# Windowed attention and a two-product feed-forward block: the first product of nine of the twelve pairs of token blocks as seven products of half sums, and two pairs at once while the weights arrive

## The chip, the cores and the metric

One core of one Trainium2 chip runs the whole program. The metric is device time of the program in microseconds. Three runs of the kernel before gave 628.5, 630.02 and 631.56 us, median 630.02 us. One further execution was profiled; all rows below come from it.

## The reference, cut to what matters

```python
# 4 batches, 8 heads, 768 tokens, head size 64; d_model 512, d_ff 2048; all float64 weights, float32 q, k, v
scores = q @ k.T / 8 - slope[h] * dist          # kept: 8 global columns and the 96 tokens up to the row's own
a = exp(scores - max); a = a / (sum(a) + 1e-9)
x = (a @ v)                                     # 4 * 768 = 3072 tokens of 512
h = x @ w_in                                    # 512 -> 2048
g = where(h >= 1, h, where(h <= -1, 0, (h + 1)**2 / 4))
out = g @ w_out                                 # 2048 -> 512, float32
```

## The kernel before, in words

The 3072 tokens are 24 units of 128; two units are a pair (c = 0 to 11, 256 tokens). Units 0 to 3 are the first blocks of the four batches; they see only themselves and go through a float32 path (`first_scores` to `first_x`). The other 20 units look at two blocks of 128 keys and go through a float16 path in two halves of four heads each (`put_unit`).

Every float16 product is made of three: an operand is the sum of a high and a low float16 part, and high*high, high*low and low*high are summed in PSUM.

The weights are float64 in memory. Each of 32 pieces (16 of `w_in`, 16 of `w_out`, 128 columns or rows of d_ff each) is loaded raw, turned into float32 by three integer steps on VectorE (`w_bits`, L480, L484, L487), split by two steps of ScalarE (`w_hi` L500, `w_scale` L507) and one of GpSimd (`w_lo` L514).

`ffn1(c, g)` is the first product of a pair: for a group g of 256 columns of d_ff (eight groups), 24 matmuls with a weight block of 128x128 and 256 moving columns (tokens), L885. `gelu(c, g, s)` makes g of it in five steps on 512 columns: ScalarE L898, VectorE L903 and L908, ScalarE L912, GpSimd L916. `ffn2(c, t, f)` is a step of the second product: three matmuls of 512 moving columns for token block t and piece f of `w_out` (L928), 32 steps a pair. `finish` scales and stores the result. `scores` (24 matmuls, L757) and `attend` (24, L800) are the attention products of half a unit; transposes of units 4 to 23 are done by DMA (`turn_p`, `turn_x`).

All work is put in a plan with `at(time, function, ...)`, and the list `PLACE` gives the order in which the functions are issued; each engine runs its instructions in that order. `PLACE` leaves some planned fillers out: a filler (`warm`, L443) is a matmul of zeros with 512 columns that nobody reads. 109 of them are issued, up to 74 us. In the order of before, pair 0's first product runs while `w_in` arrives, pair 0's second and pair 1's first while `w_out` arrives, and then, pair by pair, the second product of pair c is interleaved with the first of pair c + 1 and the attention of two units of a later pair. The 128 `check_reduce` of the weights (L546) are spread over the second half. Checks on the value ranges end in a flag that chooses a general path.

## Time and profile before

| | |
|---|---|
| median of three runs | 630.02 us |
| span of the profiled execution | 629.1 us |
| what lies around the span, by the median | 0.9 us |
| TensorE busy | 615.7 us, 98% of the span |
| VectorE, ScalarE, GpSimd busy | 448.0, 418.7, 239.5 us |
| granted clock of TensorE over the span | 0.999 |

"Busy" counts an instruction from its start to its modelled end, so that matmuls which follow each other overlap; the distance from one start to the next is what a matmul costs in a stream. The same holds for VectorE and ScalarE, whose instructions overlap by some 0.1 us.

### The profile page before, as it was taken

The page shows a single profiled execution, that of the slowest core. Times are in us where ns is not written, and L with a number is a line of the kernel's source. Part 1 is how long each engine was busy: PE and PEld are TensorE (multiplying, and loading weights), DVE is VectorE, ACT ScalarE, POOL GpSimd, SP SyncE. Part 2 cuts the span into 40 slices and gives each one's busy share as a digit, 9 for nine tenths or more (in the row PEclk, how much of TensorE's full clock was granted, in tenths as well). Part 3 has the DMA queues.
Part 4 walks back from the last instruction along what each step waited for, and adds up shares of the span by engine and source line. Part 5 has one row for each costly group of instructions (what it writes and reads, how often), then busy time and mean ns, then how long its engine had stood idle before and what let it go on. Part 6 is the DMA issues. An engine that isn't in the chain of part 4 may idle for free. (4 is left out here: it accounts for less than half of the span.)

```text
span 629.1 us, 14881 instructions
## 1 busy us (share of the span) xinstructions
PE 615.7 (98%) x5665; PEld 420.8 (67%) x5665; DVE 448.0 (71%) x1150; ACT 418.7 (67%) x1070; POOL 239.5 (38%) x226
## 2 busy tenths in 40 slices
PE   7999999899999999999999999999999999999996
PEld 4676666556876767767757667667667767767652
DVE  6889999987676656665777777777777686663440
ACT  4778898997777776676686776766866765632220
POOL 0336786650544424433443333425324421122210
PEclk9999999999999999999999999999999999999999
DMA  6847566597533553464395497586476455361121
GB/s 201 261 144 225 187 227 221 129 170 157 126 87 77 91 121 93 80 148 111 69 231 154 94 208 186 127 186 175 110 177 183 112 140 137 76 150 69 51 69 38
DMA packets 144227, 88.08 MB, mean 140 GB/s; under 512 B 108180, under 2 KB 124820, under 8 KB 144148
## 3 DMA queue, kind: packets, MB, share of 16 engines
q1 hardware_dynamic: 144000, 86.92, 55.4%
q8 instruction: 46, 0.75, 0.5%
q14 instruction: 33, 0.27, 0.1%
q10 hardware_dynamic: 148, 0.13, 0.1%
HBM read 54.53 MB, written 6.29 MB: 97 GB/s over the span
## 5 line engine op out<-in xcount | busy, mean ns | idle before, releaser
L885 PE MATMUL h<-xt,wih 128*128 128x256 f16 x1536 | 256.4, 273 | 1.0 <-DVE u L908 0.9
L916 POOL TENSOR_TENSOR gl<-u,gh 128x512 f16<-128x512 f32 x96 | 117.4, 1224 | 284.9 <-ACT gh L912 274.6
L885 PE MATMUL h<-xt,wil 128*128 128x256 f16 x768 | 209.4, 273 | 0.0
L885 PEld LDWEIGHTS <-wih 128*128 128x128 f16 x1536 | 147.4, 98 | 30.9 <-DVE u L908 1.6
L928 PE MATMUL o<-wol,gh 128*128 128x512 f16 x384 | 145.6, 379 | 1.3 <-POOL wol L514 1.2
L928 PE MATMUL o<-woh,gh 128*128 128x512 f16 x384 | 145.8, 380 | 0.0
L928 PE MATMUL o<-woh,gl 128*128 128x512 f16 x384 | 145.6, 379 | 0.0
L928 PEld LDWEIGHTS <-gh 128*128 128x128 f16 x768 | 71.8, 98 | 67.3
L903 DVE SCALAR_TENSOR_TENSOR h<-h,u 128x512 f32<-128x512 f32 x96 | 66.7, 694 | 68.2 <-ACT u L898 68.0
L590 ACT ACTIVATE z<-z,nm 128x256 f32<-128x256 f32 (+1 forms) x192 | 91.7, 479 | 14.9 <-DVE nm L578 14.3
L912 ACT ACTIVATE gh<-u 128x512 f16<-128x512 f32 x96 | 60.2, 627 | 60.4 <-DVE u L908 60.1
L898 ACT ACTIVATE u<-h,half 128x512 f32<-128x512 f32 x96 | 64.9, 676 | 43.3 <-PE h L885 43.2
L578 DVE CUSTOM_DVE_ANT_0 z<-s,bias 128x256 f32<-128x256 f32 (+1 forms) x192 | 67.2, 396 | 26.6 <-PE s L757 23.2
L885 PEld LDWEIGHTS <-wil 128*128 128x128 f16 x768 | 75.0, 98 | 8.8
L775 DVE SCALAR_TENSOR_TENSOR ph<-z,ph 128x1024 f16<-128x1024 f32 x40 | 60.0, 1499 | 22.1 <-ACT ph L773 21.8
L928 PEld LDWEIGHTS <-gl 128*128 128x128 f16 x384 | 37.5, 98 | 47.2 <-issue 2.2
L908 DVE SCALAR_TENSOR_TENSOR u<-u,h 128x512 f32<-128x512 f32 x96 | 65.3, 681 | 3.3 <-DVE good L298 0.3
L546 DVE TENSOR_REDUCE sq<-c_raw 128x1 f32<-128x256 f32 x128 | 48.6, 408 | 0.2
L773 ACT ACTIVATE ph<-z 128x1024 f16<-128x1024 f32 x40 | 42.0, 1050 | 0.7
L757 PEld LDWEIGHTS <-qh 64*128 64x128 f16 x960 | 26.9, 94 | 16.7 <-issue 9.5
L800 PEld LDWEIGHTS <-pt 128*128 128x128 f16 x960 | 33.4, 98 | 7.0
L590 ACT ACTIVATION_READ_ACCUMULATOR z<-z,nm 128x1 f32 x192 | 36.0, 187 | 0.0
(101 smaller groups left out, 676.6 us busy)
## 6 DMA issues: line engine op xcount, KB each, us to landing
w_raw<-in_moe_w_in_dram SPq DMA_DIRECT2D x16, 512.0 KB, 3.8
w_raw<-in_moe_w_out_dram SPq DMA_DIRECT2D x16, 512.0 KB, 3.7
c_raw<-in_moe_w_in_dram SPq DMA_DIRECT2D x32, 256.0 KB, 3.5
c_raw<-in_moe_w_out_dram SPq DMA_DIRECT2D x32, 256.0 KB, 3.1
vr<-in_v_dram SPq DMA_DIRECT2D x28, 256.0 KB, 3.5
kr<-in_k_dram SPq DMA_DIRECT2D x28, 256.0 KB, 3.7
qr<-in_q_dram SPq DMA_DIRECT2D x24, 256.0 KB, 4.0
out_dram<-ob SPq DMA_DIRECT2D x23, 256.0 KB, 3.0
```

The costliest lines, as they stand in the source:

```text
L546: nc.vector.tensor_reduce(sq[:, col : col + 1], tops[n, e], axis=AX.X, op=op, apply_absolute_value=True)
L578: nc.vector.tensor_tensor_reduce(out=p32[u, hf][:, hh, :], in0=pts[u, hf][hh // 2][:, hh % 2, 0:n], in1=bias[:, 4 * hf + hh, base : base + n],
L590: nc.scalar.activation(z, z, AF.Exp, bias=nm[:, c : c + 1], scale=-1.0, accum_out=sums[:, c : c + 1])
L773: nc.scalar.activation(phs[u, hf][:, 0, :], zf, AF.Copy, scale=SP_)
L775: nc.vector.scalar_tensor_tensor(phs[u, hf][:, 1, :], zf, SP_, phs[u, hf][:, 0, :], op0=ALU.mult, op1=ALU.subtract)
L885: nc.tensor.matmul(hp[:, e, :], w[:, dc, f], xt[:, hf, 2 * a + j, :], start=(n == 0), stop=(n == 3 * NDC - 1),)
L898: nc.scalar.activation(us[c, g], hs[c, g], AF.Relu, bias=half, scale=2.0 / (SV * SW), accum_out=su[:, col : col + 1])
L903: nc.vector.scalar_tensor_tensor(ws[c, g], hs[c, g], 4.0 / (SV * SW), us[c, g], op0=ALU.mult, op1=ALU.max)
L908: nc.vector.scalar_tensor_tensor(dst, us[c, g], 4.0, ws[c, g], op0=ALU.min, op1=ALU.mult)
L912: nc.scalar.activation(gh, ws[c, g], AF.Copy)
L916: (nc.gpsimd if GL == "p" else nc.vector).tensor_sub(gl, ws[c, g], gt[c, g][0])
L928: nc.tensor.matmul(po, a[:, cs], w[:, f, :], start=(f == 0 and n == 0), stop=(f == NFC - 1 and n == 2))
```

## The change

- Pairs 0, 1 and 2 keep the plain first product. For pairs 3 to 11 the tokens (2 x 128), d_model (2 x 256) and each group of d_ff (2 x 128) are halved, and the product of 2x2 blocks is made of seven products (`product`, "p1" to "p7") of sums and differences of blocks, for half of the groups (four, j = 0 or 1) at a time. A product is 24 matmuls with 128 moving columns.
- The sums on the token side (`mix_x`, `split_b`) are made on GpSimd and ScalarE, and turned by DMA (`turn_b`); those on the weight side (`t_sum`, `t_mix`, `t_hi`, `t_lo`) once for all pairs.
- Partial results are kept: `keep` copies a PSUM bank to SBUF on ScalarE, `join` adds such a copy on VectorE. A half has three of each and four `gelu` of 512 columns, keyed (j, 11), (j, 12), (j, 22), (j, 21).
- Pair 1's first product runs beside pair 0's while `w_in` arrives, and the second products of both while `w_out` arrives. 45 fillers are issued instead of 109.
- The sums of the exponentials come from a 65th column of ones in `attend` instead of ScalarE's accumulator; `gelu` no longer accumulates; the low part of x is made on GpSimd, not on VectorE; `turn_p` is two transposes of half the size; the checks at the end are moved ahead of the last stores and two are new.
- Buffers: one pool of 10 tiles in place of 6 and 7, three PSUM banks for first products and results of pair 1 (two before, and one for the weights).

```diff
-NFILL = 150
+FIRSTW = 3
+PRODUCTS = ("p1", "p5", "p2", "p6", "p3", "p7", "p4")
+NFILL = 120
...
+    def product(c, j, name):
+        k = PRODUCTS.index(name)
+        x, slot, r, e = {
+            "p1": (("a", 0), "a", 0, 0), "p2": (("a", 1), "c", 1, 0), "p3": (("b", 1), "b", 1, 1),
+            "p4": (("b", 3), "a", "t", (1, 0)), "p5": (("b", 4), "b", "t", (0, 0)),
+            "p6": (("b", 0), "a", "t", (1, 1)), "p7": (("b", 2), "a", "t", (0, 1)),
+        }[name]
+        fresh = name in ("p1", "p5", "p2")
...
+        if fresh:
+            hs[c, j, slot] = ps_h.tile([P, 4, P], F32, tag="h", name=f"h{c}_{j}{slot}")
+        else:
+            after(("s", c, j, {"p6": "p1", "p7": "p6", "p3": "p5", "p4": "p7"}[name]))
+        hp = hs[c, j, slot]
+        for m in range(4):
+            g = 4 * j + m
+            n = 0
+            for dc in range(2):
+                for a, b in ((0, 0), (0, 1), (1, 0)):
+                    if r == "t":
+                        w = tt[g, e[0]][:, a, dc, e[1], :]
+                    else:
+                        f = (2 * g + e) * P
+                        w = (wil if a else wih)[:, 2 * r + dc, f : f + P]
+                    nc.tensor.matmul(
+                        hp[:, m, :], w, xf(b, dc), start=(fresh and m == n == 0),
+                        stop=(m == 3 and n == 5), skip_group_check=not fresh,
+                    )
+                    n += 1
...
+    def keep(c, j, name):
...
+        nc.scalar.activation(s, flat(hs[c, j, {"p1": "a", "p6": "a", "p5": "b"}[name]]), AF.Copy)
+        sc[c, j, name] = s
+
+    def join(c, j, t):
+        slot, name, prod = {11: ("c", "p1", "p2"), 12: ("b", "p6", "p3"), 22: ("a", "p5", "p7")}[t]
...
+        if t == 22:
+            dst = flat(ps_h.tile([P, 4, P], F32, tag="h", name=f"h{c}_{j}d"))
+            did.add(("s", c, j, "p7"))
+        nc.vector.tensor_add(dst, h, sc[c, j, name])
...
+    def mix_x(c, n):
...
+        if n == 0:
+            nc.gpsimd.tensor_add(s1, a21, a22)
+        elif n == 1:
+            nc.gpsimd.tensor_sub(a21, a11, a21)
+        elif n == 2:
+            nc.gpsimd.tensor_sub(a11, s1, a11)
+        else:
+            nc.gpsimd.tensor_sub(a12, a12, a11)
...
     for g in range(8):
+        t = tw[2 * g + 1] + 7.0
+        at(t, ffn1, 0, g)
+        put_gelu(0, g, t + 2.7)
+        t = max(t + 2.7, LAG + PA * 2 * g)
+        at(t, ffn1, 1, g)
+        put_gelu(1, g, t + 2.7)
+    for f in range(NFC):
+        t = tw[NFC + f] + 7.0
+        for c in range(2):
+            for x in range(2):
+                at(t + 0.65 * (2 * c + x), ffn2, c, x, f, f)
```

`PLACE` is a new list. From pair 6 on it repeats itself for every half: p1, p5, one `ffn2` step of the half before, `attend`, p6, a step, `scores`, p2, five steps, p7, a step, `attend`, three steps, `scores`, p3, a step, p4, four steps.

## Rows read from the trace of the kernel before

**Rows 1.** The profile's page: busy time of each engine, and TensorE's busy share and granted clock in 40 slices of the span.

```profile
PE 615.7 (98%) x5665; PEld 420.8 (67%) x5665; DVE 448.0 (71%) x1150; ACT 418.7 (67%) x1070; POOL 239.5 (38%) x226
PE   7999999899999999999999999999999999999996
PEclk9999999999999999999999999999999999999999
```

**Rows 2.** Busy time of each engine in stretches of 20 us. Columns: stretch, its length, then busy us and instructions of PE, PEld, DVE, ACT, POOL, then the granted clock, the DMA share and GB/s.

```profile
0.00:20.00 20.00, 15.91 (x62) 9.83 (x63) 14.44 (x75) 10.18 (x33) 1.88 (x7) 1.00 0.65 202
...
40.00:60.00 20.00, 19.24 (x150) 14.28 (x149) 20.00 (x48) 16.92 (x40) 11.63 (x11) 1.00 0.59 179
...
100.00:120.00 20.00, 18.15 (x197) 12.35 (x196) 19.69 (x45) 18.89 (x47) 14.36 (x13) 1.00 0.51 144
...
300.00:320.00 20.00, 20.00 (x198) 13.95 (x196) 14.11 (x36) 14.81 (x39) 11.11 (x10) 1.00 0.53 119
...
460.00:480.00 20.00, 20.00 (x210) 13.48 (x208) 16.39 (x44) 14.31 (x37) 6.24 (x6) 1.00 0.73 183
```

**Rows 3.** TensorE's timeline from 300 to 312 us: start, duration, what. One group of `ffn1` (300.98 to 303.60), three steps of `ffn2`, `scores`, the next group, and `attend`.

```profile
300.98 0.38 PE L885 MATMUL h<-xt,wih 128*128 128x256 f16 x2
...
303.60 0.38 PE L928 MATMUL o<-woh,gh 128*128 128x512 f16 x1
...
304.25 0.38 PE L928 MATMUL o<-woh,gh 128*128 128x512 f16 x1
...
305.33 0.38 PE L928 MATMUL o<-woh,gl 128*128 128x512 f16 x1
305.64 0.84 PE L757 MATMUL s<-kh,qh 64*128 64x128 f16 x24
306.42 0.39 PE L885 MATMUL h<-xt,wih 128*128 128x256 f16 x2
...
310.34 0.86 PE L800 MATMUL av<-vh,pt 128*128 128x64 f16 x24
311.04 0.38 PE L928 MATMUL o<-woh,gh 128*128 128x512 f16 x1
```

**Rows 4.** TensorE's groups by shape: count, then busy us, mean ns of one, and idle time before them.

```profile
L885 PE MATMUL h<-xt,wih 128*128 128x256 f16 x1536 | 256.4, 273 | 1.0 <-DVE u L908 0.9
L885 PE MATMUL h<-xt,wil 128*128 128x256 f16 x768 | 209.4, 273 | 0.0
L800 PE MATMUL av<-vh,pt 128*128 128x64 f16 x960 | 34.5, 193 | 0.0
L443 PE MATMUL spare<-zeros 128*128 128x512 f16 x109 | 30.5, 413 | 0.0
L885 PEld LDWEIGHTS <-wih 128*128 128x128 f16 x1536 | 147.4, 98 | 30.9 <-DVE u L908 1.6
```

**Rows 5.** TensorE's timeline from 34.66 us: the float32 path of half a unit, and fillers.

```profile
34.66 0.60 PE L616 MATMUL tp<-ident,z 128*128 128x128 f32 x4
35.19 0.71 PE L567 MATMUL s<-kr,qr 64*128 64x128 f32 x8
35.84 0.61 PE L443 MATMUL spare<-zeros 128*128 128x512 f16 x2
36.28 1.00 PE L634 MATMUL av<-vr,pt 128*128 128x64 f32 x8
37.12 1.03 PE L443 MATMUL spare<-zeros 128*128 128x512 f16 x4
37.98 0.38 PE L656 MATMUL xtp<-ident,x 128*128 128x128 f32 x2
```

**Rows 6.** VectorE's timeline from 116.10 us, with the third step of the last weight piece at 117.90.

```profile
116.10 0.42 DVE L578 CUSTOM_DVE_ANT_0 z<-s,bias 128x256 f32<-128x256 f32 x1
...
116.45 0.69 DVE L484 SCALAR_TENSOR_TENSOR w_bits<-w_raw,w_bits 128x512 int32<-128x512 int32 x1
117.05 0.93 DVE L740 COPY kh<-kg 128x256 f16<-128x256 f16 x1
117.90 0.69 DVE L487 SCALAR_TENSOR_TENSOR w_f<-w_raw,w_bits 128x512 int32<-128x512 int32 x1
118.52 0.15 DVE L602 TENSOR_SCALAR r<-sums 128x4 f32<-128x4 f32 x1
118.77 1.23 DVE L775 SCALAR_TENSOR_TENSOR ph<-z,ph 128x1024 f16<-128x1024 f32 x1
119.91 0.42 DVE L578 CUSTOM_DVE_ANT_0 z<-s,bias 128x256 f32<-128x256 f32 x1
```

**Rows 7.** TensorE's timeline: the second matmul, at 121.87, of the first step of `ffn2` that reads the last weight piece; and the last matmul of all.

```profile
121.39 0.38 PE L928 MATMUL o<-woh,gh 128*128 128x512 f16 x1
121.87 0.38 PE L928 MATMUL o<-wol,gh 128*128 128x512 f16 x1
...
623.11 0.38 PE L928 MATMUL o<-woh,gl 128*128 128x512 f16 x1
```

**Rows 8.** Groups of ScalarE and VectorE by shape, as in rows 4: the instructions nearest to `keep`, and those nearest to `join`.

```profile
L898 ACT ACTIVATE u<-h,half 128x512 f32<-128x512 f32 x96 | 64.9, 676 | 43.3 <-PE h L885 43.2
L903 DVE SCALAR_TENSOR_TENSOR h<-h,u 128x512 f32<-128x512 f32 x96 | 66.7, 694 | 68.2 <-ACT u L898 68.0
L816 DVE TENSOR_TENSOR xh<-x,xh 128x256 f16<-128x256 f32 x40 | 19.4, 486 | 0.6 <-ACT xh L814 0.6
```

More of the change, by code (lines that the diff above doesn't have):

```diff
@@ L40 @@
 SC = SQK * SQK
+VMAX = 6.0e7
+VSPAN = 256.0
 NQKV = 3 * NU - B
@@ L318, in to_f32, with fast_path @@
     nc.vector.scalar_tensor_tensor(dst, lo, 29, t, op0=ALU.logical_shift_right, op1=ALU.bitwise_or)
-def fast_path(ctx, tc, q, k, v, nraw, nval, w_in, w_out, out, half, nm, sums, sq, su):
+def fast_path(ctx, tc, q, k, v, nraw, nval, w_in, w_out, out, half, nm, rr, sq, worst):
     nc = tc.nc
@@ L399, in distances @@
     def distances(own):
+        after("positions")
+        did.add(("dist", own))
         n = P if own else WIN
@@ new lines, in ffn2 @@
+    def ffn2(c, t, f, n):
+        if c < FIRSTW:
+            g, e = divmod(f, 2)
+            key, cs = g, slice(e * CH + t * P, e * CH + (t + 1) * P)
+        else:
+            j, m = divmod(f, NFC // 2)
+            m, e = divmod(m, 2)
+            key, cs = (j, 10 * (t + 1) + e + 1), slice(m * P, (m + 1) * P)
+        after(("w", NFC + f), ("g", c, key, 4))
+        if n == 0:
+            p, tag = (ps_h, "h") if c == 1 else (ps_o, "o")
+            os_[c, t] = p.tile([P, DM], F32, tag=tag, name=f"o{c}_{t}")
+        gh, gl = gt[c, key]
+        for i, (a, w) in enumerate(((gh, woh), (gh, wol), (gl, woh))):
+            nc.tensor.matmul(
+                os_[c, t], a[:, cs], w[:, f, :], start=(n == 0 and i == 0), stop=(n == NFC - 1 and i == 2)
+            )
+        if n == NFC - 1:
@@ L966, in fast_path, with put_gelu, put_finish @@
+    def put_gelu(c, g, t):
+        for s, d in enumerate((0.1, 0.8, 1.5, 2.2, 2.8)):
+            at(t + d, gelu, c, g, s)
+    def put_finish(c, t, x):
+        at(t, finish, c, x, 2 if c + 1 == NCH and x else 1)
     at(0.0, positions)
@@ new lines, in fast_path @@
+    starts = {2: T2}
+    if FIRSTW == 3:
+        for g in range(8):
+            t = T2 + 2.7 * g
+            at(t, ffn1, 2, g)
+            put_gelu(2, g, t + 2.7)
+        starts[3] = T2 + 22.0
+        for f in range(NFC):
+            for x in range(2):
+                at(starts[3] + 1.4 * f + 0.65 * x, ffn2, 2, x, f, f)
+        for x in range(2):
+            put_finish(2, starts[3] + 22.6, x)
+    for g in range(8):
+        put_mix(g, TT[g])
+    J0 = 2 * FIRSTW
+    tj = {J0: starts[FIRSTW]}
@@ new lines, in fast_path @@
+    for J in range(J0, 2 * NCH):
+        first = J == J0 and FIRSTW == 2
+        tj[J + 1] = tj[J] + (11.5 if first else PJ)
+    for c in range(FIRSTW + 1, NCH + 1):
+        starts[c] = tj[2 * c]
+    for J in range(J0, 2 * NCH):
+        c, j = divmod(J, 2)
+        t, dt = tj[J], (tj[J + 1] - tj[J]) / 7
+        for n, name in enumerate(PRODUCTS):
+            tp = t + dt * n
+            at(tp, product, c, j, name)
+            if name in ("p1", "p5", "p6"):
+                at(tp + 1.5, keep, c, j, name)
+            d = {"p2": 11, "p3": 12, "p7": 22, "p4": 21}.get(name)
+            if d:
+                if d != 21:
+                    at(tp + 1.6, join, c, j, d)
+                put_gelu(c, (j, d), tp + 2.2)
+        last = J + 1 == 2 * NCH
+        t, dt = tj[J + 1] + 1.5, 0.66 if last else PJ / 16
+        order = [(x, e, m) for x in range(2) for e in ((0, 1) if x == 0 else (1, 0)) for m in range(4)]
+        for n, (x, e, m) in enumerate(order):
+            at(t + dt * n, ffn2, c, x, 8 * j + 2 * m + e, 8 * j + n % 8)
+            if j == 1 and n % 8 == 7:
+                put_finish(c, t + dt * n + 0.8, x)
```

730 lines of the change are left out of this document (385 added, 345 removed), and 302 rows, old and new, of the table PLACE.

## The prediction

> **What bounds the kernel now.** The page comes first: TensorE is busy for 98% of the span, in nearly every slice, at full clock, and no other engine passes 71% [rows 1]. The reader is to see from this that work taken from TensorE is worth its time, wherever TensorE lacks nothing. Whether it lacks something is told by the stretches of 20 us [rows 2]: from 300 to 320 and from 460 to 480 us TensorE is busy throughout, with VectorE at 14.1 and 16.4 of 20. From 40 to 60 us VectorE is busy for all of 20.00, and for 19.69 from 100 to 120 us, and there TensorE's busy time is in part fillers, which are no work, 109 of them [rows 4]. So the kernel has two stages: until the last weight piece is in, VectorE sets the pace, and after it TensorE.
>
> The price of TensorE's work is read from the timeline as distances between starts [rows 3]. A group of `ffn1`: 300.98 to 303.60, 2.62 us, 109.2 ns for each of 24 matmuls. A step of `ffn2`: from 303.60 to 305.33 are eight matmuls, 216.3 ns each, 0.649 us a step. `scores`: the last matmul before ends at 305.33 + 0.22 = 305.55, the next group starts at 306.42, 0.87 us. `attend`: 310.34 to 311.04, 0.70 us. The float32 path of half a unit [rows 5]: 0.53, 0.65 and 0.84 us for tp, s and av, and about 0.27 for the two transposes xtp (half of tp's four, an estimate), 2.29 us together.
>
> The whole of before, in these prices: 96 groups, 251.5 us; 384 steps, 249.2; 40 `scores`, 34.8; 40 `attend`, 28.0; 8 float32 halves, 18.3; 109 fillers of 0.216, 23.5. That is 605.3 us. The last matmul ends at 623.11 + 0.22 = 623.3 [rows 7], so TensorE stood idle for 18.0 us in all. Where? The first step that needs the last weight piece runs its second matmul at 121.87, 0.48 us after the first instead of 0.22: it waits for that piece [rows 7]. The order puts ahead of it 15 groups (39.3), 31 steps and a matmul (20.3), the float32 path (18.3), all fillers (23.5), 3 `scores` (2.6), an `attend` (0.7): 104.7 us. So 17.2 of the 18.0 us of idle time lie before 121.87. From there the kernel runs at TensorE's speed.
>
> **The change, part by part.** *Seven products.* A plain pair costs 8 groups, 192 matmuls of 256 columns, 21.0 us. A changed pair costs 2 x 7 x 24 = 336 matmuls of 128 columns. The trace has no float16 matmul of 128 columns over all 128 rows, so its price is bounded: 29.2 ns from below (`attend`, 64 columns: 0.70 us / 24) and 109.2 ns from above (256 columns) [rows 3]. The rise is 0.417 ns a column between 64 and 256 and 0.418 between 256 and 512 columns, one straight line through three points; on it 128 columns cost 55.9 ns. I take that: 18.8 us a pair, 2.2 saved, 19.9 in nine pairs. A product is 1.34 us.
>
> Each of these matmuls has a weight block of its own, and a weight load shows 98 ns [rows 4]. But `attend` loads one too for each of its 24 matmuls and still starts one every 29 ns [rows 3], so loads overlap and don't set the pace at 56. The Trainium skill ("TensorE: Matmul & The Clock Gate", section "Back-to-back issue gap") speaks against the change here: it gives about 81 ns a matmul for a sustained stream of loads and matmuls at 128 columns. By that figure the sum below would be some 76 us more. The row of `attend` contradicts it in a short burst; that no burst of 24 at 128 columns is in the trace is why it stays among the rivals.
>
> *The rest of TensorE's list.* 24 plain groups, 62.9 us; 126 products, 169.0; 384 steps, 249.2; `scores` and `attend` as before, 62.8 (a 65th column in `attend` is 40 x 24 x 0.4 ns = 0.4, left out); float32 path 18.3; 45 fillers 9.7. Together 571.9 us, 33.4 less than before.
>
> *The start.* What TensorE may lack is set by VectorE's order. In before the third step of the last weight piece starts at 117.90 [rows 6]. In the new order the worst place that I find is piece 24 (the ninth of `w_out`). Ahead of its third step stand, against what stood ahead of 117.90: 80 weight steps for 95 (-15 x 0.60 = -9.0); 32 steps of `gelu` for 26 (+3.6), because pair 1 now runs beside pair 0; 22 masks of attention for 8 (+14 x 0.345 = +4.8); 5 low parts of the probabilities for 1 (+4 x 1.14 = +4.6); 3 more `scale_x` (at the mask's 0.345, +1.0), one more split of v (+0.6), 2 `t_lo` (+1.2), 4 small `norm` steps (at 0.25, +1.0), 2 copies of global keys or values (at 0.85, +1.7). All prices are distances of starts in [rows 6]; 0.60 is L484 to the next. The sum is +9.5 us, so 127.4. From the third step to the matmul that uses the piece went 121.87 - 117.90 = 4.0 us; 131.4. TensorE's list ahead of it: 16 groups (41.9), 32 steps (20.8), float32 path (18.3), fillers (9.7), 6 `scores` (5.2), 4 `attend` (2.8): 98.7 us. So TensorE has stood idle for 32.7 us by then, where before it was 17.2 at 121.87. So two pairs beside the weights bring no gain of their own: TensorE's idle time and fillers together are 32.7 + 9.7 = 42.4 us for 17.2 + 23.5 = 40.7. VectorE was the limit of this stage, and the change gives it more to do there, not less. Bounds of the idle time: 17.2 if the order hides what it adds, and some 45 if VectorE's added work is slowed as the copy at 117.05 is (0.85 us, while a step on twice the columns takes 0.60).
>
> *The steady part on other engines.* A pair gets 6 `keep` and 6 `join`. By the nearest rows [rows 8] a `keep` is 0.68 us and a `join` 0.69 (from below the 0.49 of xh). ScalarE loses its accumulator reads; VectorE loses four xh. A pair takes 48.0 us of TensorE before (21.0 + 20.8 + 4 x 1.57), 45.8 after. At 16.4 of 20 [rows 2] VectorE has 39.4 us of work in 48.0; +4.1 - 1.9 gives 41.6 in 45.8, 91% at the busiest stretch. GpSimd had 6 to 11 of 20 there and takes the sums. TensorE hides all of this, as long as it never waits; if the cover were gone, the joins alone are 54 x 0.69 = 37 us. That ScalarE is queued behind a `keep` delays exponentials, which have a half of slack. The transposes rise from 80 to 109 smaller ones on SP's queue; their reader is always one or more products later, and I cost them at nothing; a late one would show as a wait of `attend` or of p5, some us each. The checks are issued with some 65 us of TensorE work still to come: nothing.
>
> **Sum.** 571.9 + 32.7 of idle time + 0.8 as before = 605.4 for the last matmul. Behind the last matmul the span has 629.1 - 623.3 = 5.8 us, unchanged, and the median lies 0.9 above the span: 612.1 us. Against 630.0 that is -17.9: 33.4 of work saved, 15.5 given back at the start.
>
> **Rivals.** (a) *The start is no worse than before.* Idle stays 17.2: 596.6 us. For it: GpSimd and ScalarE have room from 40 to 60 us [rows 2]. Against: VectorE has none, and the count above. 10%.
>
> (b) *The drain of PSUM banks takes the pace* (the slower side). Three banks serve a half that needs four results and three copies. p6 writes on p1's bank, and only p5, a step and `attend` lie between (2.7 us), for a `keep` of 0.68 in ScalarE's queue. p5 takes the bank that the (j, 12) result leaves: behind p3 a step, p4, four steps and p1 (5.9 us) cover a join and three `gelu` steps (4 x 0.69 = 2.8 us plus their queues). VectorE's longest instruction, 1.23 us, and a run of four masks stand in such queues [rows 6]. It decides from 17.9 / 18 = 1.0 us of waiting in a half; with 1.3 us at each of the two places it is 18 x 2.6 = 47 us: 659. For it: VectorE near 91%. Against: before, TensorE ran without a gap through the same kinds of queues [rows 2]. 20%, of which 4 points stay faster, 6 no change, 10 slower.
>
> (c) *Weight loads set the pace of the products.* It decides from 55.9 + 17.9 us / 3024 = 61.8 ns a matmul; at the load's 98 ns [rows 4] it costs 127 us: 739. Against: `attend`. 3%. The rule of the Trainium skill above is this rival, with 612 + 76 = 688.
>
> (d) *The clock falls.* 45 fillers for 109, none behind the first group. In the first 20 us TensorE was busy for 15.9 and kept the full clock [rows 2]; in the new order it has 98.7 us of work in 131. If a stretch of 20 us ran at half clock, its 16 us of work would take 32, some 12 more than the stretch has: 624. 6%.
>
> (e) The flag picks the general path, or the products are not run: 1%.
>
> **How the numbers follow.** Forecast 612 with 60%, its own range 602 to 622. Less than 0.5% (3.2 us) can't be told from no change. Faster: 60 + 10 + 6 + 4 = 80%; no change 6%; slower 10 + 3 + 1 = 14%. The range goes from 594, just below (a), to 634, which takes in the first part of (b) and leaves out its rest, (c) and (e).
>
> **What would show it.** Products at about 56 ns a matmul, 1.34 us each; above 62 the saving is gone. The ninth piece's first step of `ffn2` near 131 us, with VectorE full from 40 us on; near 116 would be (a). From some 150 us on no idle time ahead of p5, p6 and p4; if there is any, ended by ScalarE's `keep` or VectorE's `gelu`, it is (b). Granted clock 1.00 throughout. The last matmul near 605 us. The prediction is wrong if the steady part takes more than 47 us a pair, or if the idle time of the start is below 20 or above 45 us.

## The result, and the profile after

The changed kernel takes 637.74 us (median of 4 runs, 636.59 to 638.58) against 630.61 us for the kernel before (4 runs in between): ratio 1.0118, 95% interval 1.0094 to 1.0143. It is slower, by 1.2%; 612 was forecast. The profiled execution spans 635.5 us.

The profile's page after, busy time and slices, answers to [rows 1]:

```profile
PE 592.3 (93%) x6897; PEld 420.7 (66%) x6897; DVE 475.8 (75%) x1186; ACT 429.2 (68%) x864; POOL 365.0 (57%) x371
...
PE   5997999759999999999999999999999949998996
...
PEclk9998899869999999999999999999999998999999
```

TensorE's share fell from 98 to 93%. Its slices name two places: the first 150 us, and slice 32, where nothing had been low. The stretches of 20 us answer to [rows 2] (busy time of PE, PEld, DVE, ACT, POOL with instruction counts, then the granted clock, DMA share and GB/s):

```profile
40.00:60.00 20.00, 17.45 (x141) 14.38 (x139) 19.21 (x51) 16.78 (x46) 13.22 (x13) 0.91 0.54 171
...
80.00:100.00 20.00, 20.00 (x206) 14.73 (x204) 20.00 (x43) 19.43 (x41) 16.57 (x18) 1.00 0.62 154
100.00:120.00 20.00, 18.01 (x176) 11.25 (x173) 15.19 (x35) 15.58 (x33) 16.96 (x19) 0.91 0.79 214
120.00:140.00 20.00, 11.14 (x86) 5.22 (x81) 19.42 (x45) 16.09 (x32) 13.06 (x15) 0.80 0.82 209
300.00:320.00 20.00, 20.00 (x297) 15.90 (x295) 16.46 (x40) 16.49 (x34) 11.00 (x14) 1.00 0.94 205
460.00:480.00 20.00, 20.00 (x261) 14.34 (x260) 16.61 (x42) 14.95 (x29) 14.58 (x13) 1.00 0.74 158
500.00:520.00 20.00, 16.15 (x224) 11.62 (x220) 7.65 (x24) 4.82 (x9) 5.33 (x8) 1.00 0.27 68
520.00:540.00 20.00, 15.64 (x219) 12.68 (x220) 15.47 (x38) 13.58 (x23) 8.81 (x7) 0.83 0.79 129
```

From 300 to 320 and from 460 to 480 us TensorE is full, as before. From 500 to 520 us every engine is idle for part of the time: something holds them all. TensorE's timeline around one product answers to [rows 3]:

```profile
301.19 1.50 PE L972 MATMUL h_0b<-xtb,tt 128*128 128x128 f16 x24
302.53 1.50 PE L972 MATMUL h_0a<-xtb,tt 128*128 128x128 f16 x24
303.87 0.28 PE L972 MATMUL h_0c<-xta,wih 128*128 128x128 f16 x2
```

From 301.19 to 302.53 and to 303.87: 1.34 us a product, 55.9 ns a matmul. From scores(16, 1) at 368.07 to scores(18, 1) at 413.99, one pair of the steady part, are 45.9 us; 45.8 were forecast, and before it was 48.0.

In the prediction's prices the listed work of TensorE is 571.8 us. The last matmul ends at 629.18 + 0.22 = 629.4, so TensorE stands idle for 57.6 us, not for 33.5. At any place of the order the idle time so far is the start read from the trace less the work listed ahead of it. So "idle" is a remainder: what a matmul takes beyond its price, at a lower clock for one, counts in it too. These differences give the account that everything below refers to:

| stretch | idle time before | forecast | measured | where it is read |
|---|---|---|---|---|
| to attend(7, 1) | 18.0 | 32.7 | 41.2 | starts at 179.4 |
| from there to scores(23, 0) | 0 | 0.8 for all that follows | 2.8 | starts at 515.9 |
| to attend(22, 1) | 0 | | 10.1 | starts at 536.0 |
| to the last matmul | 0 | | 3.5 | ends at 629.4 |
| all | 18.0 | 33.5 | 57.6 | |

The forecast of 612.1 is missed by 25.6 us. Beside the 24.1 us of idle time, the span ends 6.1 instead of 5.8 us behind the last matmul, and the median lies 2.2 instead of 0.9 us above the span.

**The late gaps.** GpSimd's timeline (start, duration, line, tiles, in brackets the idle time before) around 513 and 562 us:

```profile
507.04 0.73 POOL L841 TENSOR_TENSOR xs<-xs 128x256 f32<-128x256 f32 x1
513.60 0.37 POOL L1071 PARTITION_ALL_REDUCE spread<-spread  x1 [5.83 <-issue]
520.65 0.71 POOL L843 TENSOR_TENSOR xs<-xs 128x256 f32<-128x256 f32 x1 [6.68 <-issue]
...
562.51 0.38 POOL L256 PARTITION_ALL_REDUCE anybad<-worst  x1 [5.82 <-DVE worst L1106]
569.79 0.72 POOL L837 TENSOR_TENSOR xs<-xs 128x256 f32<-128x256 f32 x1 [6.90 <-issue]
```

An all-reduce is 0.37 us in the record, but GpSimd does nothing else from 507.8 to 520.7 us. The groups of the lines L1071 and L843 (engine, instruction, count, ns of one, first and last start) show what its sequencer, POOLq, does meanwhile:

```profile
L1071 POOLq MODIFY_POOL_CONFIG  x2: 14/14/14, 507.7 to 507.7; - x2
L1071 POOL PARTITION_ALL_REDUCE spread<-spread x1: 371/371/371, 513.6 to 513.6; - x1
```

```profile
L843 POOLq MODIFY_POOL_CONFIG  x2: 82/82/83, 513.9 to 514.0; - x2
```

Two MODIFY_POOL_CONFIG stand at the beginning of each gap, 5.9 us ahead of the all-reduce and 6.7 ahead of the next sum. So the time goes to the change from ordinary work to the all-reduce and to the change back. Behind it stands the last sum of pair 10's inputs (`mix_x`, L843), and ScalarE and TensorE stand behind that. Their timelines:

```profile
521.40 1.27 ACT L851 ACTIVATE xb<-xs 128x1280 f16<-128x1280 f32 x1 [14.92 <-POOL xs L843]
```

```profile
524.36 1.46 PE L756 MATMUL s<-kh,qh 64*128 64x128 f16 x23 [8.21 <-DVE nm L559]
```

The second all-reduce is that of the flag (`anybad`): the verdict is issued in the middle of the stream, and the all-reduce follows it there. Pair 11's sums wait behind it.

**The start.** TensorE's waits around the place that the prediction named, its timeline:

```profile
131.56 1.06 PE L800 MATMUL av<-vh,pt 128*128 128x65 f16 x22 [3.70 <-DMA pt<-ph]
134.94 0.58 PE L1039 MATMUL o<-woh,g 128*128 128x512 f16 x1 [2.31 <-ACT woh L451]
137.09 0.59 PE L1039 MATMUL o<-wol,g 128*128 128x512 f16 x1 [1.57 <-POOL wol L462]
137.47 1.06 PE L1039 MATMUL o<-woh,g 128*128 128x512 f16 x2
```

134.94 is ffn2(1, 0, 8), the first step on piece 24, forecast at 131.4. VectorE's timeline shows why it is late:

```profile
102.82 0.70 DVE L1012 SCALAR_TENSOR_TENSOR h<-h,u 128x512 f32<-128x512 f32 x1 [2.22 <-ACT u L1010]
...
119.39 0.70 DVE L1012 SCALAR_TENSOR_TENSOR h<-h,u 128x512 f32<-128x512 f32 x1 [2.45 <-ACT u L1010]
...
132.57 0.68 DVE L438 SCALAR_TENSOR_TENSOR w_f<-w_raw,w_bits 128x512 int32<-128x512 int32 x1
```

The last row is the third step of piece 24: 132.57, forecast 127.4. VectorE had not run without gaps up to there: it waited 2.22 and 2.45 us for relus of pair 1's groups. Against the kernel before up to 117.90, VectorE's busy time up to this step rose from 107.1 to 116.1 us, by 9.0 where 9.5 were forecast, and its idle time from 10.8 to 16.5.

The second of these waits is in part the clock's. Stretches of TensorE at a granted clock of 0.50, 1.2 GHz, and the rows around the group of ffn1 that the relu waits for, ffn1(1, 6):

```profile
114.90:118.30 3.40, 3.40 (x18) 2.46 (x17) 2.04 (x5) 2.11 (x5) 3.40 (x4) 0.50 0.16 60
132.00:142.20 10.20, 6.31 (x28) 2.43 (x25) 9.67 (x22) 8.08 (x17) 6.42 (x8) 0.50 1.14 301
```

```profile
114.17 0.39 PE L935 MATMUL h<-xt,wih 128*128 128x256 f16 x2 [1.99 <-DVE w_f L438]
...
118.47 0.89 PE L800 MATMUL av<-vh,pt 128*128 128x65 f16 x24
118.67 0.69 ACT L1010 ACTIVATE u<-h,half 128x512 f32<-128x512 f32 x1 [1.63 <-PE h L935]
```

From 114.17 to 118.47 the group took 4.30 us instead of 2.62. The granted clock was also 0.50 from 53.5 to 56.9 and from 63.7 to 67.1 us, 20.5 us in all before 142.2; in the kernel before it was 1.00 all that time.

### The profile page after: what moved, and what is told of

It is laid out like the page before. It is cut to its first block, busy times and chain, and to the rows that moved or that the text cites. A ratio compares the mean times of both kernels' runs of the same rounds, so it can differ in the third digit from the quotient of the medians.

```text
span 635.5 us, 17333 instructions
## 1 busy us (share of the span) xinstructions
PE 592.3 (93%) x6897; PEld 420.7 (66%) x6897; DVE 475.8 (75%) x1186; ACT 429.2 (68%) x864; POOL 365.0 (57%) x371
## 4 chain that ended last, share of the span: by engine, by line
PE 69%; POOL 11%; DVE 7%; issue 6%; ACT 4%; DMA 2%; SPq 0%; POOLq 0%; DVEq 0%; ACTq 0%
PE o L1039 29%; PE h_0a L972 7%; PE h_1a L972 7%; PE h_0b L972 4%; PE av L800 4%; PE h_1b L972 4%; PE s L756 4%; PE h L935 3%; POOL tsum L512 3%; PE h_0c L972 2%; POOL tsum L503 2%; PE h_1c L972 2%; POOL wol L462 1%; PE spare L399 1%; PE av L613 1%
## 5 line engine op out<-in xcount | busy, mean ns | idle before, releaser
L1039 PE MATMUL o<-wol,gh 128*128 128x512 f16 x352 | 133.9, 381 | 0.0
L1039 PE MATMUL o<-woh,gl 128*128 128x512 f16 x352 | 133.9, 380 | 0.0
L972 PEld LDWEIGHTS <-tt 128*128 128x128 f16 x1728 | 100.8, 98 | 12.4 <-DVE u L1014 1.4
L972 PEld LDWEIGHTS <-wih 128*128 128x128 f16 x864 | 67.5, 99 | 9.5 <-DVE u L1014 1.6
L935 PE MATMUL h<-xt,wih 128*128 128x256 f16 x384 | 68.6, 285 | 2.3 <-DVE w_f L438 2.0
L559 DVE CUSTOM_DVE_ANT_0 z<-s,bias 128x256 f32<-128x256 f32 x160 | 65.2, 415 | 7.1 <-PE s L756 6.5
L1039 PEld LDWEIGHTS <-gl 128*128 128x128 f16 x352 | 34.6, 98 | 42.1 <-issue 0.8
L935 PE MATMUL h<-xt,wil 128*128 128x256 f16 x192 | 54.6, 284 | 0.0
L935 PEld LDWEIGHTS <-wih 128*128 128x128 f16 x384 | 38.7, 102 | 9.8 <-DVE w_f L438 2.7
L756 PE MATMUL s<-kh,qh 64*128 64x128 f16 x960 | 35.0, 219 | 9.5 <-DVE nm L559 9.5
L756 PEld LDWEIGHTS <-qh 64*128 64x128 f16 x960 | 27.6, 95 | 23.2 <-DVE nm L559 10.2
L972 PEld LDWEIGHTS <-wil 128*128 128x128 f16 x432 | 42.6, 99 | 0.0
L800 PE MATMUL av<-vh,pt 128*128 128x65 f16 x960 | 36.2, 194 | 5.1 <-DMA pt<-ph 4.9
```

Of the source, the lines that this page charges most:

```text
L559: nc.vector.tensor_tensor_reduce(out=p32[u, hf][:, hh, :], in0=pts[u, hf][hh // 2][:, hh % 2, 0:n], in1=obias[hf][:, hh, :] if own else bi ...
L756: nc.tensor.matmul(pair[r][:, j, e * P : (e + 1) * P], qf[rows, a, 2 * hf + j, :], kf[rows, c, 2 * hf + j, :], start=(n == 0), stop=(n == 2),)
L800: nc.tensor.matmul(av[:, hh, :], pt[:, a, hh, kt, :], vt[:, c, 4 * hf + hh, :], start=(n == 0), stop=(n == 5),)
L935: nc.tensor.matmul(hp[:, e, :], w[:, dc, f], xt[:, a, dc, :], start=(n == 0), stop=(n == 3 * NDC - 1))
L972: nc.tensor.matmul(hp[:, m, :], w, xf(b, dc), start=(fresh and m == n == 0), stop=(m == 3 and n == 5), skip_group_check=not fresh,)
L1039: nc.tensor.matmul(os_[c, t], a[:, cs], w[:, f, :], start=(n == 0 and i == 0), stop=(n == NFC - 1 and i == 2))
```

## The experiments

All times stand beside runs of the kernel before on the same chip; ratios are to those. "The end version" is e1_spread_end. An idle time comes from the one profiled execution of a run. How far two executions differ is seen where the order up to attend(7, 1) is the same: 41.2, 39.4 and 40.8 us in the changed kernel, e1 and g2, and 18.0 and 15.9 in the kernel before and e2. A difference of 2 us in the idle time of the start says nothing by itself.

**The all-reduces.** First, both moved behind the work:

```diff
+    put(("v_spread", 1), behind=("gelu", NCH - 1, (1, 21), 4))
+    put(("verdict",), behind=("v_spread", 1))
```

> The changed kernel with the all-reduce of the check on v moved from the middle of pair 9 to behind the last low part of the last gelu, the verdict behind it; nothing is left out. Theory A (the all-reduce holds GpSimd from 507.8 to 520.7 us, and the 10 us of TensorE idle time between 515.9 and 536 are that): no such stall, idle time at the last attention near 44 us instead of 54, time 637.7 - 10 = 627 to 629 us. Rival B (the stall there is the queue of ScalarE behind split_b and would come without the all-reduce): 636 to 639 us, the same wait near 520 us. Rival C (the all-reduce is only moved to a place where it costs as much): the stall goes, but the span ends more than 6.1 us behind the last matmul, by the 13 us of the all-reduce with what lies around it: 632 to 640 us.

623.74 us, ratio 0.9909 (0.9878 to 0.9939): faster than the kernel before by 1%, and some 14 us below the changed one. The idle time stays at 42 us from 366 us to the end; both late gaps are gone, the 10.1 and the 3.5 us. The tail grows from 6.1 to 7.4 us. GpSimd's timeline at the end:

```profile
603.56 1.16 POOL L1023 TENSOR_TENSOR gl<-u,gh 128x512 f16<-128x512 f32 x1 [0.19 <-ACT gh L1021]
610.58 0.37 POOL L1071 PARTITION_ALL_REDUCE spread<-spread  x1 [5.87 <-issue]
613.36 0.37 POOL L256 PARTITION_ALL_REDUCE anybad<-worst  x1 [2.40 <-DVE worst L1106]
```

The first still has its 5.87 us in front, with two MODIFY_POOL_CONFIG at 604.9; the second, right behind it, has none of these and only 2.40 us, which end with VectorE's `worst`, its input. Theory A holds, and its price was too low by the second all-reduce, which it left out.

Does an all-reduce cost that much anywhere? In the kernel before:

```diff
+            if (f, args) == (scores, (22, 1)):
+                nc.gpsimd.partition_all_reduce(probe, probe, channels=P, reduce_op=bass_isa.ReduceOp.max)
```

> The kernel before with one all-reduce of two columns over the partitions on GpSimd added ahead of scores(22, 1), its result unused. Theory A (an all-reduce in the middle of the stream costs this kernel what it costs the changed one): 630.6 + 10 = 637 to 643 us, with a gap on GpSimd of some 12 us around it and a wait of TensorE behind it. Rival B (the order around it has enough slack): 629.5 to 632.5 us.

630.41 us, ratio 1.0000 (0.9983 to 1.0017): no change, as rival B has it. GpSimd's timeline there:

```profile
515.71 1.16 POOL L916 TENSOR_TENSOR gl<-u,gh 128x512 f16<-128x512 f32 x1 [6.24 <-ACT gh L912]
523.51 0.37 POOL L1038 PARTITION_ALL_REDUCE probe<-probe  x1 [6.64 <-issue]
530.83 3.39 POOL L916 TENSOR_TENSOR gl<-u,gh 128x512 f16<-128x512 f32 x3 [6.95 <-ACT u L898]
```

GpSimd is held for as long (6.64 and 6.95 us), but behind it stand only low parts of gelus, three at once, and they have that much slack. So what counts is what is queued behind. The changed kernel, with its all-reduce 13 places later, behind the sums:

```diff
+    put(("v_spread", 1), behind=("split_b", 10, 1))
```

> The changed kernel with the all-reduce 13 places later in the order, behind split_b(10, 1), so that the sums and low parts of pair 10's inputs stand ahead of it on GpSimd and not behind it; still in the middle of the stream. Theory A2 (the all-reduce costs nothing by itself; what costs is what is queued behind it on GpSimd, the last sum of x, on which ScalarE, the transposes and p5 wait): no wait of ScalarE for xs near 520 us, at most 1 to 3 us of TensorE's idle time there, 624 to 628 us. Rival U (GpSimd is held for some 13 us wherever it stands, and the low parts of the gelus behind it are as urgent): 632 to 639 us.

627.18 us, ratio 0.9957 (0.9942 to 0.9973): theory A2. The idle time is 43.7 us at attend(23, 1), against 43.1 at 246 us: the gap of 10.1 us is gone, though GpSimd is held as before (6.14 us ahead of the all-reduce, 7.84 behind). Some 4 us at the second all-reduce, which was left in place, remain. So what was queued behind GpSimd is shown to be the cause of the late gaps: the same all-reduce costs 10.1 us ahead of the last sum and nothing that shows behind it.

**The start: order of the pieces.** These two runs change the issue order alone. Pieces 24, 25, 26 in their own order:

```diff
+    for f, *s in steps:
+        at_ = sorted(order.index(names.index((f, n, *s))) for n in (24, 25, 26))
+        for n, m in zip((24, 25, 26), at_):
+            order[m] = names.index((f, n, *s))
```

> The changed kernel with weight pieces 24, 25 and 26 handled in that order (it handles 25 and 26 first): each of their seven steps takes the places in the queues that the three pieces have now. Theory D (the start is set by where piece 24 stands in VectorE's queue): its third step starts near 127 us instead of 132.6, TensorE's idle time at 145 us is some 36 instead of 40.7, time 632 to 635 us. Rival E (the sum of VectorE's work sets the start, not its order): the wait moves to piece 25 or 26, idle time 39 to 42, time 636.5 to 639 us.

> e1_spread_end and e3_piece24 together (the bits stay in PSUM). Theory D (the place of piece 24 costs about 3 us of the start, whatever the all-reduce does later): 623.7 - 3.5 = 619 to 621.5 us, idle time at attend(7, 1) 36 to 37 us instead of 39.4. Rival P (gains of two edits of the order don't add up in queues that run in order): 622.5 to 626 us.

e3: 634.16 us, ratio 1.0075 (1.0049 to 1.0102), idle time at attend(7, 1) 38.2 instead of 41.2. f1, on the end version: 623.16 us, ratio 0.9893 (0.9867 to 0.9920), idle time 40.8 against 39.4. By their times the first speaks for theory D, the second for rival P; the place of piece 24 is worth between 0 and 4 us. The 38.2 of e3 are only 1.2 below the lowest of the three executions with the old start, and the granted clock was 0.50 for 13.7 us before 200 us in e3, 17.1 in f1, 20.5 in the changed kernel: part of the gain of e3 may be the clock's.

**The start: the clock.** Matmuls with zeros in TensorE's waits:

```diff
+    def fill(t, n, **kw):
+        for _ in range(n):
+            nc.tensor.matmul(t, zeros, zeros[:, 0 : t.shape[2]].unsqueeze(1).to_broadcast(list(t.shape)), **kw)
...
+        fill(av, 34 * ((u, hf) == (5, 1)), start=True, stop=True)
```

> The changed kernel with TensorE's long waits of the first 137 us filled by matmuls with zeros that change nothing (32 in two av tiles, 18 ahead of ffn1(1, 6), 6 in scores(6, 1), 34 in attend(5, 1), 10 ahead of ffn2(1, 0, 8)). Theory F (the clock costs part of the start: matmuls at half clock from 53.5 to 56.6, 63.5 to 67.0, 114.8 to 118 and 137.1 to 142.2 us lose some 1.5 + 1.7 + 1.6 + 2.6 us): granted clock 1.00 from 40 to 120 us and above 0.95 from 140 to 160 us, idle time and fill together at 146 us 3 to 7 us lower, time 631 to 635 us. Rival G (TensorE waits for the weights behind each stretch anyway, so what the clock takes comes out of a wait): the clock rises, the time stays at 636 to 640 us.

640.66 us, ratio 1.0197 (1.0130 to 1.0263): no gain. Whether it is slower than without is not clear; the interval overlaps that of the changed kernel (1.0094 to 1.0143), and one of the four runs took 647.13 us. The fill is 12.6 us of work; the idle time at attend(6, 0), fill included, is 44.5 instead of 40.7. Stretches and one row of TensorE's timeline:

```profile
40.00:60.00 20.00, 16.58 (x148) 14.16 (x146) 18.01 (x49) 16.10 (x42) 12.33 (x12) 1.00 0.49 151
60.00:80.00 20.00, 17.90 (x156) 15.13 (x156) 16.08 (x32) 15.11 (x35) 11.72 (x12) 0.83 0.50 169
...
120.00:140.00 20.00, 19.59 (x197) 12.85 (x195) 15.19 (x35) 12.66 (x25) 14.38 (x15) 0.97 0.59 143
```

```profile
117.00 3.25 PE L406 MATMUL h<-zeros 128*128 128x256 f16 x18 [2.00 <-DVE w_f L442]
```

The clock rose from 0.80 to 0.97 between 120 and 140 us, and fell from 0.91 to 0.83 between 60 and 80. The last row shows a flaw of the experiment: this fill waited for the same PSUM bank as the work and then ran behind the wait, 3.0 us of it, in part at half clock. So the fill brings nothing (nearest to rival G), but it doesn't measure what the clock alone costs. Theory F's estimate of 7.4 us lost at half clock is neither confirmed nor refuted: the clock stays an open cause of the start's loss.

**The start: VectorE's waits.** Pair 1's two outputs hold two of the three banks of `ps_h`; the bits of the pieces and the groups of ffn1 share the third. Bits in SBUF:

```diff
+            if num >= NFC:
+                p, tag = mid, "m"
...
+            f = t if num >= NFC else mid.tile([P, *hi.shape[1:]], I32, tag="m", name=f"w{num}_f32")
```

> As e1_spread_end, and the bits of the w_out pieces (16 to 31) are put together in the SBUF tile of the piece instead of a PSUM bank. Theory J (pair 1 holds two of the three banks of ps_h with its outputs, so the bits and ffn1(1, 7), ffn1(1, 6) take turns on the third; VectorE's waits of 2.2 and 2.5 us before L1012 and TensorE's 2.0 us before ffn1(1, 6) are that): these waits shrink, piece 24's third step starts 3 to 5 us earlier, idle time at attend(6, 0) 34 to 36 us instead of 38.8, time 619 to 621 us. Rival K (the bank's turn hides behind VectorE's other work, or the steps become slower beside GpSimd in SBUF): 622.5 to 626 us.

638.87 us, ratio 1.0145 (1.0127 to 1.0164): 15 us slower than the end version, worse than either theory. VectorE's groups from 80 to 160 us (busy time, mean ns of one), first the changed kernel, then this one:

```profile
L435 DVE SCALAR_TENSOR_TENSOR w_bits<-w_raw,w_bits 128x512 int32<-128x512 int32 x15 | 10.3, 685 | 0.1
L438 DVE SCALAR_TENSOR_TENSOR w_f<-w_raw,w_bits 128x512 int32<-128x512 int32 x15 | 10.1, 673 | 0.0
```

```profile
L440 DVE SCALAR_TENSOR_TENSOR w_bits<-w_raw,w_bits 128x512 int32<-128x512 int32 x13 | 13.0, 1001 | 0.0
L437 DVE SCALAR_TENSOR_TENSOR w_bits<-w_raw,w_bits 128x512 int32<-128x512 int32 x13 | 12.0, 923 | 0.1
```

The steps of a piece became up to half as long again; from 60 to 170 us the three steps together take 11 us more of VectorE than in the end version. Rival K had named this and undervalued it. The edit also keeps the SBUF tile of a piece in use for longer; what that adds is not known.

> As e1_spread_end, with pieces 24, 25, 26 in that order, and the four later steps of the gelus of pair 1's groups 7 and 6 put behind the steps of pieces 21 and 25 (bits still in PSUM). Theory L (VectorE's 4.7 us of waiting behind the relus of these groups is order alone): VectorE does the pieces in that time, piece 24's third step starts some 8 us earlier than 132.6, time 617 to 620 us. Rival J again (the bits need the bank that these very groups hold, so VectorE waits at the next piece instead): 620 to 624 us, as piece 24's order alone gives, and VectorE's wait stands ahead of L429.

The kernel that ran here had the bits in the SBUF tile, as in e5, not in PSUM as the text says; so it tests the order of the pieces and of the gelu steps on top of e5, and theory L as written stays untested. 639.47 us, ratio 1.0146 (1.0129 to 1.0163): no gain there either.

The same waits taken away with the bits in PSUM, by ffn1(1, 6) ahead of pair 1's first output (f2), and that with the order of e3 (f3):

```diff
+    put(("ffn1", 1, 6), behind=("w_bits", 19, 2))
+    for s, key in enumerate([("gelu", 1, 4, 3), ("w_bits", 20, 1), ("w_bits", 20, 2), ("w_hi", 20), ("w_lo", 20)]):
+        put(("gelu", 1, 6, s), behind=key)
+    for x, key in ((0, ("ffn1", 1, 7)), (1, ("gelu", 1, 7, 1))):
+        for f in (2, 1, 0):
+            put(("ffn2", 1, x, f, f), behind=key)
```

> As e1_spread_end, with ffn1(1, 6) and its gelu moved ahead of the first ffn2 step of pair 1 (behind piece 19), and the first three steps of each of pair 1's two outputs behind ffn1(1, 7); so the outputs of pair 1 take two banks of ps_h only when ffn1(1, 6) has left its own. Theory J (the turn of one bank makes VectorE wait 2.2 and 0.8 us for relus and TensorE 1.7 us): these waits go, piece 24's third step starts 2 to 4 us earlier than 131.6, idle time at attend(7, 1) 35 to 38 us, time 619 to 622 us. Rival Q (VectorE then does two gelu steps earlier and the pieces behind them later, and waits elsewhere): 622.5 to 627 us.

> f1_spread_24 and f2_pull_16 together. Theory D with J (two separate causes): 615 to 619 us, idle time at attend(7, 1) 32 to 35 us. Rival Q: no better than f1_spread_24, 619 to 624 us.

f2: 627.26 us, ratio 0.9956 (0.9937 to 0.9976); f3: 623.60 us, ratio 0.9903 (0.9878 to 0.9927). Idle time at attend(7, 1) 45.7 and 41.4. TensorE's waits in f3 from 80 to 240 us (sum, times, longest):

```profile
PE o L1039 <- POOL wol L462: 5.9, 5, 2.6
PE av L800 <- DMA pt<-ph: 2.1, 1, 2.1
```

VectorE's waits for the relus fell from 4.7 us (f1) to 0.4, but the time stayed: TensorE now waits for the low parts that GpSimd makes, and VectorE's waits for the high parts of the weight sums (`tt`) went from 7.1 to 9.4 us (80 to 240 us). That is rival Q, in the time and in the waits.

**The start: GpSimd.** The weight sums of the first group later (e8), and the subtractions of the sums left out, on the end version (h1) and on f3 (h2):

```diff
-        getattr(nc, TMIX).tensor_sub(dst, x, y)
```

> As e1_spread_end, with the nine steps of the first group of weight sums (t_sum, t_mix, t_hi, t_lo of group 0) moved from ahead of piece 24 to ahead of the second group's. Theory N (the sums on GpSimd and their raw buffer hold up wol of pieces 22 to 24 and the load of piece 24): the idle time at attend(6, 0) falls by 2 to 4 us, time 620 to 622 us. Rival O (GpSimd and the ring have room there): 622.5 to 625 us.

> e1_spread_end with the subtractions of t_mix left out (32 instructions on GpSimd, 0.6 to 1.2 us each; the products p4 to p7 then use unmixed sums). Theory W (GpSimd's weight sums hold up the start: the low parts of the pieces, wol, stand behind them): idle time at attend(7, 1) 35 to 38 us instead of 39.4, time 619 to 622 us. Rival X (VectorE's queue sets the start, and GpSimd has room): 622.5 to 625 us. If it comes below 618 us, the sums cost more than the start shows, somewhere behind 180 us.

> f3_pull_24 with the subtractions of t_mix left out, as in h1_no_mix. In f3_pull_24 VectorE's waits for the relus of pair 1 were gone, but TensorE waited five times, 5.9 us, for wol from GpSimd, and its idle time stayed at 41.4 us. Theory W2 (VectorE and GpSimd bound the start together, so relief of one alone shows nothing): idle time at attend(7, 1) 33 to 37 us, time 615 to 619 us, more than 3 us below h1_no_mix or f3_pull_24. Rival X2 (the sums don't matter here): 622 to 625 us.

e8: 629.55 us, ratio 0.9999 (0.9984 to 1.0014), 6 us worse than the end version: VectorE then waits 5.4 us for `tt` from 80 to 160 us (2.0 in the end version). h1: 623.24 us, ratio 0.9898 (0.9867 to 0.9930): rival X. h2: 621.33 us, ratio 0.9867 (0.9837 to 0.9897), idle time at attend(7, 1) 38.3. In time h2 lies 2.3 us below f3, and h1 0.5 below the end version: some relief where VectorE's waits are gone too, none that shows where they aren't. That is the direction of theory W2, less than it asked for, and not shown: the intervals of f3 and h2 overlap, and the granted clock was 0.50 for 20.5 us before 200 us in f3, for 10.2 in h2, so that the clock may have given the difference.

**The start: attention behind the weights.** Everything of units 6 and later 100 places back (e7), or 60 places back with all weight sums behind the last piece (f4; only the shift, which both have, is shown):

```diff
+        if f in far and u >= (3 if f in ("mix_x", "split_b", "turn_b") else 6):
+            return m + min(SHIFT, max(0, (1030 - m) // 2))
```

> As e1_spread_end, with everything of units 6 and later that stands in the order ahead of the last weight piece moved about 100 places back (the shift fades out over the next 200 places). Theory H (what VectorE does for units 6 to 8 ahead of the weights, some 14 us, sets the start): the last weight piece is done 8 to 14 us earlier than 154 us, idle time at attend(7, 1) is 27 to 33 us instead of 39.4, time 612 to 618 us. Rival M (the work comes back: pair 3's products p1 and p5 wait for units 6 and 7): waits of TensorE between 175 and 230 us, time 621 to 630 us.

> As e7_units_late but 60 places back instead of 100, and all weight sums (t_sum, t_mix, t_hi, t_lo of all eight groups) in one row behind the last weight piece, each VectorE step some places behind what it waits for. Theory H (in e7 the gain was lost because sums came ahead of the last pieces on GpSimd: TensorE waited 9.2 us for wol): no wait of TensorE for wol above 2 us, idle time at attend(7, 1) 30 to 36 us, time 614 to 620 us. Rival M (the sums then come late and pair 3's product p5 waits for them, or for units 6 and 7): a wait of TensorE of 3 us or more between 195 and 230 us, time 622 to 635 us.

e7: 639.30 us, ratio 1.0137 (1.0117 to 1.0157), idle time 51.3 at attend(7, 1) and 58.2 at scores(11, 0). f4: 648.47 us, ratio 1.0310 (1.0279 to 1.0342), and TensorE waits 14.0 us in three places for `gl`. Theory H falls both times: the work comes back, as rival M says, at a higher price than either rival M gave, and in f4 on GpSimd.

**The start of the kernel before, with the products.** Up to ffn1(2, 0) its order (pair 0 alone beside the weights, 109 fillers), from there the changed kernel's; the weight sums in a row beside pairs 1 and 2 (g1), spread further (g3), or begun earlier (g4). The new lists `PLACE` are left out here:

```diff
-            p, tag = (ps_h, "h") if c == 1 else (ps_o, "o")
+            p, tag = ps_o, "o"
```

> The changed kernel with the start of the kernel before: up to ffn1(2, 0) the work is issued in the order of the kernel before (pair 0 beside the weights, pair 1 behind it, 109 fillers, two more where the order has them), from there in the order of the changed kernel; the weight sums in one row beside pair 1 and pair 2; the all-reduce at the end as in e1_spread_end. Theory R (the products are worth their 19.9 us of TensorE work, and what is missing in e1_spread_end is the price of the start with two pairs): idle time and fillers together at attend(7, 1) some 41 us as before, instead of 39.4 + 9.7 = 49, time 630 - 19.9 + 2 to 4 of later waits and tail = 611 to 615 us. Rival S (the start costs the same either way, since the sums of the weights and the changed pools come in both): 620 to 626 us. Rival T (sums, pair 1 and pair 2 collide at the seam): waits ahead of p5 of pair 3, 626 to 640 us.

> As g1_products_alone, with the 72 steps of the weight sums spread evenly from the last weight piece to just ahead of p5 of pair 3's second half (there they stood in a denser row, and GpSimd was busy for 17.1 and 19.2 of 20 us from 120 to 160 us while TensorE waited for qh and xs). Theory R (the start of the kernel before costs no more than there; what g1 lost, it lost between 140 and 220 us): idle time at scores(5, 0) 14 to 18 us as in g1, at attend(8, 1) below 27 us instead of 36, time 612 to 624 us. Rival T (pairs 1 and 2, their attention and the sums don't fit on VectorE and ScalarE there in any order): idle time at attend(8, 1) 32 to 40, time 630 to 638 us.

> As g3_sums_spread, with the weight sums beginning 85 places earlier, beside the last weight pieces, and ending 35 places earlier. Theory R: 612 to 624 us, within 4 us of g3_sums_spread. Rival V (sums ahead of the last pieces hold up the pieces' loads and low parts, as the two-pair start showed with its first group): idle time at scores(5, 0) above 20 us, and slower than g3_sums_spread by 4 us or more.

g1: 636.47 us, ratio 1.0109 (1.0063 to 1.0154); g3: 634.46 us, 1.0067 (1.0046 to 1.0089); g4: 631.81 us, 1.0026 (1.0008 to 1.0044). In g3 the idle time is 14.4 us at scores(5, 0), no more than before (17.6, and 15.4 in e2), and then rises to 30.1 at attend(7, 1) and 38.1 at the end. Its stretches:

```profile
120.00:140.00 20.00, 19.32 (x219) 11.63 (x213) 15.47 (x40) 14.57 (x29) 19.44 (x20) 1.00 0.61 122
140.00:160.00 20.00, 14.33 (x139) 7.52 (x138) 14.36 (x36) 12.52 (x26) 19.44 (x17) 0.83 0.47 85
```

GpSimd is full, TensorE is not. Theory R falls in its time, and rival T comes out in the times of g1 and g3; rival V holds for g4's start (22.0 us at scores(5, 0)), though not for its time. So in these three orders a start with one pair doesn't save what the start with two pairs loses: with fillers, g3 has 38.1 + 23.5 = 61.6 us of TensorE's time without work, the end version 42.1 + 9.7 = 51.8.

## Why the prediction was wrong

**The work: right.** A product takes 1.34 us and a pair of the steady part 45.9 us, for 1.34 and 45.8 forecast. (The total of 571.8 us is the same list in the same prices, and no reading of its own.) Of the 33.4 us that left the list, 13.8 are fillers, which are no work; 19.6 are the products' gain (the prediction's 19.9 without its rounding). Rival (c) is out. The Trainium skill ("TensorE: Matmul & The Clock Gate", section "Back-to-back issue gap") gives some 81 ns for such a stream; the trace shows 55.9 ns in 24 matmuls and in the next 24, and the measurement decides.

**The steady part: right within 2 us.** From 179 to 516 us there are 2.8 us of idle time; the waits that the trace lists from 180 to 505 us, 1.5 us, stand ahead of `attend`, none ahead of a product. Rivals (b) and, with 41.2 us at the start, (a) are out. In the list of before one step too many was counted ahead of 121.87 (the trace has 91 matmuls of `ffn2` there, not 94), so some 0.2 us of its idle time lie behind, not 0.8; it changes little.

**The checks: the step that failed.** "The checks are issued with some 65 us of TensorE work still to come: nothing." I looked at who reads the verdict, and not at what is queued behind the two all-reduces on GpSimd, where the change had put the sums of the inputs. In the kernel before the only one stands behind all that work, at 613.38 us. The sentence fits the flag's all-reduce alone, which cost 3.5 us; the dearer one, of the check on v, is issued with some 100 us of work still to come, and no term of the sum had it. e1 gives the price, 14 us in the time and 10.1 + 3.5 in TensorE's idle time. g2 shows that the place decides, e2 that the same instruction costs nothing where only slack work stands behind it. None of the rivals held this, so the slower side got its 14% for other reasons.

**The start: mis-sized.** 32.7 us forecast; 41.2 measured, and 39.4 and 40.8 in two more executions of the same start. The sum of VectorE's work (127.4) counted what VectorE does, and that rightly (9.0 us more for 9.5), and not what it waits for: third step at 132.57, 5.2 us late, of which 2.22 + 2.45 are the waits for relus shown above. The 4.0 us from there to TensorE had been read to the second matmul of a step, the first that takes the low part; that one starts at 137.09, 4.5 us behind the third step, with waits for woh and for wol ahead of it. From 137.47 to 142.17 come eleven matmuls at 0.43 instead of 0.216 us, at a granted clock of 0.50, which is 2.3 us more. "Granted clock 1.00 throughout" was wrong as well: rival (d), which got 6%, came true in 20.5 us of the start, in four pieces. Its part goes beyond the 2.3 us, since ffn1(1, 6) at half clock made VectorE wait longer, but how much of the 8.5 us it is no run separates. What I named as the bound, VectorE alone, does not survive: with its waits for the relus gone (f3) GpSimd's low parts stand in the same place, and with GpSimd relieved too (h2) 38.3 us still remain. The weight sums, of which the forecast counted two `t_lo`, are eight groups' work, most of it on GpSimd, that has to go somewhere ahead of p5; every order tried that moved them or the attention away (e7, e8, f4) paid for it later. That the start is bound by several queues that wait for one another, and by the clock, is argued from these runs and not shown; the share of each stays open, and so does whether a better order exists.

**The sum.** With 13.6 us for the all-reduces the forecast would have been 626 us for the changed kernel; the rest to 637.7 is 8.5 at the start, 2.0 in the steady part and 1.6 behind it. The best complete versions, e1, f1 and f3 (623.7, 623.2 and 623.6 us), are faster than the kernel before by 1%, where 3% had been forecast.

## What to carry to other kernels

An instruction whose result nobody needs soon is not free: price the time for which its engine is taken, the gaps on both sides included, and name what is queued behind it. A bound read as the sum of one engine's work is a lower one; in a stage where several engines are nearly full (here 20.00, 19.43 and 16.57 of 20 us from 80 to 100 us), add the waits that they have for one another, or take them from the trace of the nearest stage. Idle time read from a single execution has a spread of its own; look for runs that share the stage before believing 2 us. And when work moves to an engine with room, look again at everything that was harmless there while the queue was slack.
